# Score products in an attention kernel: operands stacked by copies over 128 rows, or used in place as two heads in the two halves of the array's rows

## The chip, the cores and the metric

One core of one Trainium2 chip. The metric is device time of one execution in microseconds (us), the median over runs. Engines are named as the profile names them: PE is TensorE (PEld its weight loads), DVE VectorE, ACT ScalarE, POOL GpSimd, SP the engine that issues the DMAs.

## The reference, cut to what matters

```python
# q, k, v: (8 batches, 8 heads, 576, 64);  tau = 0.02
def _attn_ref(q, k, v, tau):
    scores = np.matmul(q, k.transpose(0, 1, 3, 2)) / np.sqrt(64)
    thresh = np.max(scores, axis=-1, keepdims=True) - tau
    scores = np.where(scores >= thresh, scores, -1e9)
    attn = np.exp(scores - np.max(scores, axis=-1, keepdims=True))
    attn = attn / (np.sum(attn, axis=-1, keepdims=True) + 1e-09)
    return np.matmul(attn, v)

# x: attention output as (8, 576, 512);  w_k: 512x1024, w_v: 1024x512, w_r: 512x512
def _moe_ref(x, mu_k, mu_r, w_k, w_v, w_r):
    x_prev = x shifted by one position, zero first
    xk = mu_k * x + (1 - mu_k) * x_prev
    xr = mu_r * x + (1 - mu_r) * x_prev
    k = np.maximum(xk @ w_k, 0.0)
    return sigmoid(xr @ w_r) * (k * k @ w_v)
```

The threshold keeps only scores within tau of the row's maximum, so scores must be close to full f32.

## The kernel before, in words

**Two stages that overlap.** Attention goes batch by batch and, inside a batch, by pairs of heads (a "job", 36 in all: the first batch's four pairs are taken in two halves). A job's operands lie with the two heads above each other: the 64 numbers of head 0 on partitions 0 to 63, those of head 1 on 64 to 127. `raw` holds [q (576) | the last 64 keys | k (576)] for both, 1216 columns. A job has pair units, each 128 queries of both heads (128 such units over the run), and a last unit "T" with the remaining 64 queries of both heads (32 units). When a batch's attention is there, its feed-forward part runs in chunks of 256 positions (`ffn_chunk`: L853 the product with w_k, L895 with w_r, L917 with w_v).

**A pair unit** (`softmax`): the scores of the two heads go to two PSUM tiles `s`, of which there are two in all; then for each head the negated maximum (DVE, L555), the threshold (ACT, L563), exp (ACT, L571), the mask with its row sum (DVE, L579, the last reader of `s`), the reciprocal (DVE, L590), and the normalization (POOL, L604). PE then transposes the probabilities `p` (L628), ACT or DVE copies them to `pm` and `pl` (L646, L648), and `attend` multiplies with v (L708): the two heads write the two halves of the array's columns (128*64 in the profile), over 256 or 320 columns.

**Precision.** The matrix products run in fp32r, a rounded format. A number is split: `hi` is the rounded number (ACT, L434), `lo` the remainder (POOL, L440, in two pieces), and a product is hi.hi + hi.lo + lo.hi. In the feed-forward part these are three products over 128 rows. A head's scores have only 64 rows, so before the change `operands` makes stacked copies by DMA (L459, eight per job): `st1` has hi above lo, `st2` has lo above hi. Two products over 128 rows, st1.st1 and st2.st1, then hold all terms (lo.lo too). Each of them is done for two halves z of 288 keys: 4 products per head, 8 per unit, with one weight load each (L521). The T unit (L496) uses a block-diagonal `bd` and three products over 128 rows. The first job ("plain") multiplies `raw` in f32, 64 rows, head 0 in the upper and head 1 in the lower half of the array's rows (L510). An f32 product outside of transposes has two records in the trace, an fp32r product one.

**What sets the order.** The kernel adds steps to a `Plan`, each with an engine, an estimated time `occ`, a key, and what it reads and writes. `Plan.order` simulates the engines and buffers with these estimates and always places the step that can start first (ties by key; attention steps on PE have key - 1000, so they go before feed-forward steps that are also ready). The instructions are then issued in that order; each engine runs its own in order, and waits on semaphores where data or buffers are not ready. A step that writes two tiles is placed when both are free. Number of buffers per tile are those of `sbuf`/`psum`; `raw` has two, `s` two.

Of the kernel before, what the change touches and what calls it, by code (L numbers as in the profile page):

```python
# [8 lines left out]
F32 = mybir.dt.float32  # L9
FR = mybir.dt.float32r  # L10
# [38 lines left out]
class Plan:  # L49
# [18 lines left out]
    def add(self, eng, occ, fn, reads=(), writes=(), key=0.0, lat=None, kb=0, wait=0.0):  # L68
        s = Step()
        s.soft = self.SOFT.get(eng, 0.0) if self.soft else 0.0  # L70
        s.eng, s.occ, s.fn, s.key, s.kb = eng, occ, fn, key, kb
        s.lat = occ + 0.1 if lat is None else lat
        s.idx = len(self.steps)
        s.deps, s.succ, s.allocs = set(), [], []
        s.ready = wait

        def split(x):
            return x if isinstance(x, tuple) else (x, None)

        def near(b, r):  # L80
            if r is None:
                return list(b.regions.values())
            return [b.regions[x] for x in (r, None) if x in b.regions]

        for x in reads:
            b, r = split(x)
            for w, _ in near(b, r):
                s.deps.update(w)
        for x in writes:
            b, r = split(x)  # L90
            for w, rd in near(b, r):
                s.deps.update(w)
                s.deps.update(rd)
        for x in reads:
            b, r = split(x)
            b.regions.setdefault(r, ([], []))[1].append(s.idx)
            b.users.append(s.idx)
        for x in writes:
            b, r = split(x)
            if not b.users and b.make is None:  # L100
                self.tags.setdefault(b.tag, []).append(b)
            if r is None:
                b.regions = {None: ([s.idx], [])}
            else:

                b.regions[r] = ([s.idx], [])
            b.users.append(s.idx)
        s.deps.discard(s.idx)
        self.steps.append(s)
        return s  # L110
# [107 lines left out]
def tile_threshold_attention_then_rwkv_ffn(  # L218
# [12 lines left out]
    V, A, G, PE, SY = nc.vector, nc.scalar, nc.gpsimd, nc.tensor, nc.sync  # L231
# [3 lines left out]
    P = 128  # L235
    B, NPAIR, _, _ = qk.shape
    D = P // 2
    S = out.shape[1]
# [6 lines left out]
    HS = S // 2  # L245
    KT = S
    W = 2 * S + ST
# [11 lines left out]
    add = plan.add  # L259
    DQ = 0.55  # L260
    HALF = 1
    W0, W1, W2, W3, AVK = 3.0, 3.5, 50.0, 2.0, 4.5
    PREP, PB, VB, COLD, EARLY = 8, 2, 2, 24, 30
# [3 lines left out]
    def sbuf(tag, shape, dtype=F32, bufs=1):  # L267
        return plan.buf(sb, tag, shape, dtype, bufs)
# [4 lines left out]
    def fixed(name, shape, dtype=F32):  # L273
# [13 lines left out]
        writes=[(small, 0)],  # L287
        key=-100,
# [5 lines left out]
        reads=[(small, 0)],  # L294
        writes=[(small, 1)],
        key=-100,
# [5 lines left out]
        reads=[(small, 0)],  # L302
        writes=[(small, 2)],
        key=-100,
# [104 lines left out]
    def operands(job, key):  # L409
        b, hp = job["b"], job["hp"]  # L410
        raw = job["raw"] = sbuf("raw", [P, W], F32, 2)
        add("DMA", DQ, lambda: SY.dma_start(raw.get(), qk[b, hp]), writes=[raw], key=key - PREP - 5, kb=576)
        add(
            "ACT",
            0.67,
            lambda: A.activation(raw.get()[:, 0:S], raw.get()[:, 0:S], AF.Copy, scale=small.get()[:, 2:3]),
            reads=[(small, 2)],
            writes=[raw],
            key=key - PREP,
        )  # L420
        vt = job["v"] = sbuf("v", [P, 5, P], F32, VB)
        add(
            "DMA",
            DQ,
            lambda: SY.dma_start(vt.get(), v[b, hp].rearrange("p (c n) -> p c n", c=5)),
            writes=[vt],
            key=key - 5,
            kb=320,
        )
        if job["plain"]:  # L430

            return
        hi, lo = job["hi"], job["lo"] = sbuf("hi", [P, W], FR), sbuf("lo", [P, W], FR)
        add("ACT", 1.1, lambda: A.activation(hi.get(), raw.get(), AF.Copy), reads=[raw], writes=[hi], key=key - PREP)  # L434
        for y in range(2):
            cs = slice(0, S) if y == 0 else slice(S, W)
            add(
                "POOL",
                1.41 + 0.15 * y,
                lambda cs=cs: G.tensor_tensor(  # L440
                    lo.get()[:, cs], raw.get()[:, cs], hi.get()[:, cs].bitcast(F32), op=ALU.subtract
                ),
                reads=[raw, hi],
                writes=[(lo, y)],
                key=key - PREP,
            )
        job["st"] = [(sbuf("st1", [P, W], FR, 3), sbuf("st2", [P, S], FR, 3)) for _ in range(2)]
        for h in range(2):
            sl = slice(h * D, (h + 1) * D)
            t1, t2 = job["st"][h]  # L450

            up, dn = slice(0, D), slice(D, P)
            for dst, rows, src, n, r in (
                (t1, up, hi, W, (hi, None)),
                (t2, dn, hi, S, (hi, None)),
                (t1, dn, lo, W, (lo, None)),
                (t2, up, lo, S, (lo, 0)),
            ):
                fn = (lambda dst=dst, rows=rows, src=src, n=n, sl=sl: SY.dma_start(  # L459
                    dst.get()[rows, 0:n].bitcast(F32), src.get()[sl, 0:n].bitcast(F32)  # L460
                ))
                add("DMA", DQ, fn, reads=[r], writes=[(dst, rows.start)], key=key - PREP, kb=n // 4)

    def scores(unit, ss, key):
        job, c = unit["job"], unit["c"]
        raw = job["raw"]

        def keys(y, z):
            k0 = KT + (ST if unit["kind"] == "P" and y == 0 else 0)
            return slice(k0 + z * HS, k0 + (z + 1) * HS)

        if unit["kind"] == "T" and not job["plain"]:

            hi, lo = job["hi"], job["lo"]
            for v_, src in enumerate((raw, lo)):
                for h in range(2):
                    sl = slice(h * D, (h + 1) * D)  # L480
                    add(
                        "ACT",
                        0.26,
                        lambda v_=v_, src=src, sl=sl: A.activation(
                            bd.get()[sl, v_, sl], src.get()[sl, SM:S].bitcast(F32), AF.Copy
                        ),
                        reads=[(src, None if v_ == 0 else 0)],
                        writes=[(bd, (v_, h))],
                        key=key - 3,
                    )  # L490
            prods = [(0, hi), (0, lo), (1, hi)]
            for j, (v_, r) in enumerate(prods):

                def mm(j=j, v_=v_, r=r):
                    for z in range(2):
                        PE.matmul(ss[1].get()[:, z, 0:HS], bd.get()[:, v_], r.get()[:, keys(1, z)], start=(j == 0), stop=(j == 2))  # L496

                add("PE", 0.264, mm, reads=[bd, r], writes=[ss[1]], key=key - 1000, lat=0.44)
            return
        if unit["kind"] == "T" or job["plain"]:  # L500

            last = unit["kind"] == "T"

            def both():
                for z in range(2):
                    for h in range(2):
                        hr = slice(h * D, (h + 1) * D)
                        o = ss[1].get()[hr, z, 0:HS] if last else ss[h].get()[:, z, 0:HS]
                        q = slice(SM, S) if last else slice(c * P, (c + 1) * P)
                        PE.matmul(o, raw.get()[hr, q], raw.get()[hr, keys(h, z)], start=True, stop=True)  # L510

            occ = 1.2 if last or key > COLD else 3.0
            add("PE", occ, both, reads=[raw], writes=list(ss.values()), key=key - 1000, lat=occ + 0.25)
            return
        for y in range(2):
            st1, st2 = job["st"][y]
            for j, l in enumerate((st1, st2)):

                def mm(j=j, l=l, r=st1, y=y):
                    for z in range(2):  # L520
                        PE.matmul(  # L521
                            ss[y].get()[:, z, 0:HS],
                            l.get()[:, c * P : (c + 1) * P],
                            r.get()[:, keys(y, z)],
                            start=(j == 0),
                            stop=(j == 1),
                        )

                add("PE", 0.264, mm, reads=[l, st1], writes=[ss[y]], key=key + 0.5 * y - 1000, lat=0.44)

    def softmax(unit):
        n = unit["n"]
# [412 lines left out]
    n = 0  # L945
# [94 lines left out]
```

## Time and profile before

| | |
|---|---|
| median of 3 runs | 1096.16 us (1094.26 to 1098.05) |
| profiled execution, first to last instruction (span) | 1096.8 us; no other time is given for it |
| PE busy, products | 1024.5 us, 93%, 6832 records |
| DVE, ACT, POOL busy | 769.9, 736.4, 580.1 us |
| score products L521 | 1008 |
| copies by DMA L459 | 280, of 448 KB (hi or lo to both tiles of a head) in two pieces of 304 and 144 KB |
| all DMA traffic | 119.62 MB |

Products on PE overlap in the records: each has its start and a modelled end, so their pace is read from the starts. Rows of "PE in order of time" give start, length from the first start to the last end, the line, the shape of weights (rows*columns), the shape of the moving operand, and how many in a row. In rows of windows, after the window and its length, stand busy us (and count) of PE, PEld, DVE, ACT and POOL, then PE's granted clock, the share of the DMA engines and GB/s.

### The profile page before, as it was taken

How to read it: one execution, taken by the hardware profiler on the slowest of the kernel's cores; microseconds unless marked ns; L12 is line 12 of the kernel's file. 1: busy time of each engine (PE TensorE's matmuls, PEld its weight loads, DVE VectorE, ACT ScalarE, POOL GpSimd, SP SyncE). 2: the span in 40 equal slices, each digit the busy share in tenths (PEclk: the TensorE clock that was granted, in tenths of full speed). 3: DMA queues.
4: the chain of work that ended last, by engine and by line, in shares of the span. 5: the costliest groups of instructions: out<-in, count | busy, mean ns of one | idle time of the engine just before them, and what ended most of it. 6: DMA issues, size and time to landing. Idle time of an engine off the chain costs nothing.

```text
span 1096.8 us, 19388 instructions
## 1 busy us (share of the span) xinstructions
PE 1024.5 (93%) x6832; PEld 848.8 (77%) x6832; DVE 769.9 (70%) x1707; ACT 736.4 (67%) x1549; POOL 580.1 (53%) x584
## 2 busy tenths in 40 slices
PE   4667889998999999999999999999999999999998
PEld 3446667776878778788788878886888878888887
DVE  5999978877878788798877858855878488322220
ACT  5766977775876768777678767865777667344442
POOL 4667766544554555456545654654455544344441
PEclk9878999999999999999999999999999999999999
DMA  9994566444444444445444434530645141000000
GB/s 282 227 343 133 138 160 172 118 103 122 103 112 112 103 121 103 113 112 135 105 115 114 108 86 113 122 91 25 143 104 133 36 99 35 20 20 20 20 20 20
DMA packets 41279, 119.62 MB, mean 109 GB/s; under 512 B 6880, under 2 KB 6880, under 8 KB 41184
## 3 DMA queue, kind: packets, MB, share of 16 engines
q1 hardware_dynamic: 41184, 118.39, 41.6%
q8 instruction: 55, 0.90, 0.3%
q14 instruction: 40, 0.33, 0.1%
HBM read 44.70 MB, written 9.44 MB: 49 GB/s over the span
## 4 chain that ended last, share of the span: by engine, by line
PE 72%; DVE 12%; ACT 6%; DMA 5%; POOL 3%; issue 2%; SPq 0%; POOLq 0%; ACTq 0%; DVEq 0%
PE w L853 16%; PE w L917 14%; PE w L708 12%; PE w L628 10%; PE s L521 10%; PE w L895 8%; DMA st<-lo 3%; DVE p L579 3%; DVE mk L810 3%; DVE sm L555 2%; PE s L496 2%; ACT p L571 2%; DMA raw<-in_qk 2%; POOL lo L440 1%; DVE sm L589 1%
## 5 line engine op out<-in xcount | busy, mean ns | idle before, releaser
L604 POOL TENSOR_SCALAR p<-p,sm 128x576 f32<-128x576 f32 x288 | 223.1, 784 | 228.7 <-DVE sm L590 129.4
L579 DVE SCALAR_TENSOR_TENSOR p<-s,sm,p 128x576 f32<-128x576 f32 x288 | 232.8, 813 | 58.6 <-ACT p L571 56.4
L853 PE MATMUL w<-xk,wk 128*128 128x256 f32 x1728 | 237.8, 286 | 1.3 <-POOL xk L831 0.9
L555 DVE TENSOR_REDUCE sm<-s 128x1 f32<-128x576 f32 x288 | 210.8, 750 | 39.7 <-PE s L521 27.6
L853 PEld LDWEIGHTS w<-xk,wk 128*128 128x128 f32 x1728 | 219.4, 190 | 3.8 <-ACT pm L646 1.4
L917 PE MATMUL w<-wv,k 128*128 128x512 f32 x864 | 220.5, 396 | 1.6 <-ACT pm L646 1.5
L628 PE MATMUL w<-ident,p 128*128 128x128 f32 x1312 | 198.2, 283 | 22.6 <-POOL p L604 21.0
L571 ACT ACTIVATE p<-s,sm 128x576 f32<-128x576 f32 x288 | 210.1, 730 | 0.5
L628 PEld LDWEIGHTS w<-ident,p 128*128 128x128 f32 x1312 | 154.3, 144 | 62.0 <-POOL p L604 38.2
L917 PEld LDWEIGHTS w<-wv,k 128*128 128x128 f32 x864 | 155.8, 188 | 30.9 <-ACT pm L646 2.4
L646 ACT ACTIVATE pm<-w 128x512 f32<-128x512 f32 x174 | 102.5, 591 | 81.1 <-PE w L628 80.0
L831 POOL TENSOR_TENSOR xk<-mk,xk 128x512 fp32r<-128x512 f32 x72 | 94.9, 1318 | 104.8 <-ACT xk L823 104.7
L708 PE MATMUL w<-pm,v 128*64 128x256 f32 (+1 forms) x1024 | 144.8, 421 | 3.5 <-DVE pm L648 3.5
L563 ACT ACTIVATE sm<-sm,small 128x1 f32<-128x1 f32 x288 | 83.6, 290 | 93.7 <-DVE sm L555 90.7
L810 DVE SCALAR_TENSOR_TENSOR mk<-m,mu_sb,xT 128x256 f32<-128x256 f32 x128 | 87.2, 721 | 77.1 <-POOL xk L831 77.1
L521 PE MATMUL s<-st 128*128 128x288 f32 x504 | 119.6, 319 | 21.3 <-DVE p L579 15.3
L876 POOL TENSOR_TENSOR k<-r,k 128x512 fp32r<-128x512 f32 x72 | 93.7, 1302 | 71.1 <-ACT k L866 71.0
L440 POOL TENSOR_TENSOR lo<-raw,hi 128x576 fp32r<-128x576 f32 x70 | 105.6, 1526 | 43.6 <-ACT hi L434 36.2
L708 PEld LDWEIGHTS w<-pm,v 128*64 128x64 f32 x1024 | 71.0, 140 | 58.7 <-issue 9.0
L521 PEld LDWEIGHTS s<-st 128*128 128x128 f32 x504 | 82.0, 193 | 40.3 <-issue 25.5
L895 PE MATMUL w<-wr,xk 128*128 128x512 f32 x432 | 110.8, 396 | 1.6 <-ACT pm L646 1.6
L521 PE MATMUL s<-st,st 128*128 128x288 f32 x504 | 111.3, 303 | 0.0
(62 smaller groups left out, 1112.1 us busy)
## 6 DMA issues: line engine op xcount, KB each, us to landing
raw<-in_qk SPq DMA_DIRECT2D x36, 608.0 KB, 5.1
st<-hi SPq DMA_DIRECT2D x70, 304.0 KB, 3.2
st<-lo SPq DMA_DIRECT2D x70, 304.0 KB, 4.2
v<-in_v SPq DMA_DIRECT2D x36, 320.0 KB, 4.3
st<-hi SPq DMA_DIRECT2D x70, 144.0 KB, 3.5
st<-lo SPq DMA_DIRECT2D x70, 144.0 KB, 4.0
out<-sg SPq DMA_DIRECT2D x32, 256.0 KB, 2.0
wk<-in_w_k SPq DMA_DIRECT2D x8, 512.0 KB, 8.8
```

Of the source, the lines that this page charges most:

```text
L440: lambda cs=cs: G.tensor_tensor(lo.get()[:, cs], raw.get()[:, cs], hi.get()[:, cs].bitcast(F32), op=ALU.subtract),
L521: PE.matmul(ss[y].get()[:, z, 0:HS], l.get()[:, c * P : (c + 1) * P], r.get()[:, keys(y, z)], start=(j == 0), stop=(j == 1),)
L555: lambda sv=sv, col=col: V.tensor_reduce(col(0), sv(), axis=AX.XY, op=ALU.max, negate=True),
L571: lambda sv=sv, pv=pv, col=col: A.activation(pv(), sv(), AF.Exp, bias=col(0)),
L579: lambda sv=sv, pv=pv, col=col: V.scalar_tensor_tensor(pv(), sv(), col(1), pv(), op0=ALU.is_ge, op1=ALU.mult, accum_out=col(2)),
L604: lambda y=y: G.tensor_scalar(p.get()[:, y], p.get()[:, y], sm.get()[:, 3, y : y + 1], 0.0, op0=ALU.mult, op1=ALU.add),
L628: PE.transpose(pt.get()[:, c, :], p.get().rearrange("p y s -> p (y s)")[:, o : o + P], ident.get())
L708: PE.matmul(o.get()[hs, 0:n], vt.get()[:, c, hs], pt[:, 0:n], start=(c == 0), stop=(c == 4))
L810: V.scalar_tensor_tensor(d.get()[:, y, o : o + n], diff.get()[:, y, o : o + n], mu_sb.get()[:, j, hc + y : hc + y + 1], prv[:, hc + y], op ...
L853: PE.matmul(h.get()[:, f], l, r, start=(ct == 0 and i == 0), stop=(ct == NCT - 1 and i == 2))
L895: PE.matmul(z.get(), l, r, start=(ct == 0 and i == 0), stop=(ct == NCT - 1 and i == 2))
L917: PE.matmul(vps.get(), l, r, start=(ft == 0 and i == 0), stop=(ft == NFT - 1 and i == 2))
```

## The change: three products over 64 rows, both heads side by side

The copies go. The scores read `hi` and `lo` where they are; for each half z of the keys, three products per head, hi.hi, hi.lo and lo.hi, alternate between head 0 (partitions 0 to 63, the upper half of the array's rows) and head 1 (the lower half): 12 products with 12 weight loads per unit instead of 8, each over 64 rows. They are two steps (one per z) that each write both heads' `s` tiles, where there were four that wrote one. `hi` and `lo` get two buffers each in place of one, and the three `st1` and `st2` go. T units, the plain job and all else are as they were; the plan is computed anew, so the order changes everywhere.

```diff
-        hi, lo = job["hi"], job["lo"] = sbuf("hi", [P, W], FR), sbuf("lo", [P, W], FR)
+        hi, lo = job["hi"], job["lo"] = sbuf("hi", [P, W], FR, 2), sbuf("lo", [P, W], FR, 2)
...
-        job["st"] = [(sbuf("st1", [P, W], FR, 3), sbuf("st2", [P, S], FR, 3)) for _ in range(2)]
-        for h in range(2):
...
-                add("DMA", DQ, fn, reads=[r], writes=[(dst, rows.start)], key=key - PREP, kb=n // 4)
...
-        for y in range(2):
-            st1, st2 = job["st"][y]
-            for j, l in enumerate((st1, st2)):
-
-                def mm(j=j, l=l, r=st1, y=y):
-                    for z in range(2):
...
-                add("PE", 0.264, mm, reads=[l, st1], writes=[ss[y]], key=key + 0.5 * y - 1000, lat=0.44)
+        hi, lo = job["hi"], job["lo"]
+        qs = slice(c * P, (c + 1) * P)
+        for z in range(2):
+
+            def mm(z=z):
+                for j, (l, r) in enumerate(((hi, hi), (hi, lo), (lo, hi))):
+                    for h in range(2):
+                        hr = slice(h * D, (h + 1) * D)
                         PE.matmul(
-                            ss[y].get()[:, z, 0:HS],
-                            l.get()[:, c * P : (c + 1) * P],
-                            r.get()[:, keys(y, z)],
+                            ss[h].get()[:, z, 0:HS],
+                            l.get()[hr, qs],
+                            r.get()[hr, keys(h, z)],
                             start=(j == 0),
-                            stop=(j == 1),
+                            stop=(j == 2),
                         )
+            add("PE", 0.48, mm, reads=[hi, lo], writes=list(ss.values()), key=key - 1000, lat=0.66)
```

In the changed kernel the line numbers behind the cut are smaller by 16: L505 is the new score product, L510 becomes L492, L496 L478, L555 L539, L579 L563, L628 L612, L708 L692, L853 L837, L895 L879, L917 L901.

On PE in mid-kernel, two score blocks that follow each other, one of either head, before (`s_2874` and `s_2888` are the score tiles, `w` a PSUM tile of another product, `xk` the mixed input of the feed-forward part):

```order
L853 MATMUL w_2870<-xk_2308,wk_0_185 128x256 x3
L521 MATMUL s_2874<-st_2_2637 128x288 x2
L521 MATMUL s_2874<-st_2_2637,st_2_2648 128x288 x2
L853 MATMUL w_2870<-xk_2308,wk_0_217 128x256 x3
L521 MATMUL s_2888<-st_1_2452 128x288 x2
L521 MATMUL s_2888<-st_1_2452,st_1_2461 128x288 x2
L853 MATMUL w_2870<-xk_2308,wk_0_321 128x256 x3
```

The two heads stand apart, each as four products over the whole array. A unit in the same stretch of the changed kernel:

```order
L837 MATMUL w_2911<-xk_2133,wk_0_617 128x256 x3
L505 MATMUL s_2930<-hi_2438 128x288
L505 MATMUL s_2932<-hi_2438 128x288
L505 MATMUL s_2930<-lo_2450,hi_2438 128x288
L505 MATMUL s_2932<-lo_2450,hi_2438 128x288
L505 MATMUL s_2930<-hi_2438,lo_2450 128x288
L505 MATMUL s_2932<-hi_2438,lo_2450 128x288
```

The six rows of L505 come a second time, for the other z, and then L837 goes on. The two heads have moved together into one block that alternates between the halves.

On SP near its start, before (`wk` pieces of w_k, `raw` the operands of a coming job):

```order
L342 DMA wk_0_100<-in_w_k 128x512
L459 DMA st_0_109<-hi_103 64x1216
L459 DMA st_0_112<-hi_103 64x576
L459 DMA st_1_117<-hi_103 64x1216
L459 DMA st_0_112<-lo_107 64x576
L459 DMA st_1_124<-hi_103 64x576
L459 DMA st_1_124<-lo_107 64x576
L412 DMA raw_129<-in_qk 128x1216
```

The copies stand between the second piece of w_k and the third load of `raw`. In the changed kernel:

```order
L342 DMA wk_0_100<-in_w_k 128x512
L342 DMA wk_0_113<-in_w_k 128x512
L412 DMA raw_121<-in_qk 128x1216
L342 DMA wk_0_133<-in_w_k 128x512
L412 DMA raw_146<-in_qk 128x1216
L342 DMA wk_0_159<-in_w_k 128x512
```

Loads of weights and operands have moved into the places of the copies.

More of the change, by code (lines that the diff above doesn't have):

```diff
@@ L446, in operands @@
             )
-        job["st"] = [(sbuf("st1", [P, W], FR, 3), sbuf("st2", [P, S], FR, 3)) for _ in range(2)]
-        for h in range(2):
[L449 to L461, printed above, removed]
-                add("DMA", DQ, fn, reads=[r], writes=[(dst, rows.start)], key=key - PREP, kb=n // 4)
     def scores(unit, ss, key):
```

## The prediction

> **What bounds the kernel now.** I read the page first (engines, slices, chain), then the busy time by stages, then PE's waits, then PE in order of time.
>
> ```profile
> PE 1024.5 (93%) x6832; PEld 848.8 (77%) x6832; DVE 769.9 (70%) x1707; ACT 736.4 (67%) x1549; POOL 580.1 (53%) x584
> DMA  9994566444444444445444434530645141000000
> PE 72%; DVE 12%; ACT 6%; DMA 5%; POOL 3%; issue 2%; SPq 0%; POOLq 0%; ACTq 0%; DVEq 0%
> 0.00:10.00 10.00, 1.85 (x8) 1.18 (x8) 0.58 (x5) 3.93 (x4) 0.70 (x6) 1.00 0.75 261
> 10.00:60.00 50.00, 31.79 (x160) 22.72 (x160) 44.39 (x86) 35.39 (x72) 33.27 (x28) 0.90 0.96 263
> 60.00:110.00 50.00, 34.26 (x202) 26.40 (x198) 49.10 (x81) 31.92 (x67) 33.59 (x26) 0.83 0.73 225
> 150.00:930.00 780.00, 760.08 (x5298) 630.11 (x5297) 602.72 (x1381) 564.73 (x1232) 421.05 (x443) 1.00 0.43 108
> 930.00:1096.00 166.00, 161.72 (x967) 141.35 (x965) 38.39 (x90) 66.07 (x107) 64.86 (x60) 1.00 0.06 20
> ```
>
> The stage rows give window, length, then busy us of PE, weight loads, DVE, ACT and POOL, clock, DMA share and GB/s. Two stages differ. From 10 to 110 us the vector engine is full (44.4 and 49.1 of 50 us) and TensorE is not. From 150 us to the end TensorE is full (760 of 780, then 162 of 166), with DVE at 77% in the first of these. Busy time on PE covers modelled ends, so I check against PE's waits from 150 us on:
>
> ```profile
> PE w L628 <- POOL p L604: 4.9, 6, 1.2
> PE s L521 <- DVE p L579: 4.6, 6, 1.9
> ```
>
> These two are the largest; nothing here is waited for long. So from 150 us on, what is added to or taken from TensorE's stream is added to or taken from the time, nearly one for one, and the change must be counted on TensorE.
>
> **The products themselves.** One pair unit now has 8 score products of 288 columns, 504+504 = 1008 in 126 units. Two rows of the page have the counts; three of PE in order of time (start, length, line, count) give the pace, since products overlap and only the starts count:
>
> ```profile
> L521 PE MATMUL s<-st 128*128 128x288 f32 x504 | 119.6, 319 | 21.3 <-DVE p L579 15.3
> L521 PE MATMUL s<-st,st 128*128 128x288 f32 x504 | 111.3, 303 | 0.0
> ...
> 655.83 0.43 PE L521 MATMUL s<-st 128*128 128x288 f32 x2
> 656.09 0.43 PE L521 MATMUL s<-st,st 128*128 128x288 f32 x2
> 656.36 0.86 PE L917 MATMUL w<-wv,k 128*128 128x512 f32 x3
> ```
>
> From 655.83 to 656.36 four products start: 0.1325 us each, their weight loads hidden under the product before. Before: 126 x 8 x 0.1325 = 133.6 us.
>
> The change makes 12 products of 64 rows per unit, alternately in the upper and the lower half of the rows. Whether two of them share one step is shown by the first job, which has always worked that way (L510):
>
> ```profile
> 8.15 0.29 PEld L510 LDWEIGHTS s<-raw 64*128 64x128 f32 x2 [8.15 <-ACT raw L416]
> 8.15 0.85 PE L510 MATMUL s<-raw 64*128 64x288 f32 x2 [8.15 <-ACT raw L416]
> 8.15 1.33 PE L510 MATMUL s<-raw 64*128 64x288 f32 x4 [8.15 <-ACT raw L416]
> 8.15 2.29 PE L510 MATMUL s<-raw 64*128 64x288 f32 x8 [8.15 <-ACT raw L416]
> L510 PE MATMUL s<-raw x8: 681/684/847, 8.1 to 9.8; 64*128 64x288 f32 x8
> ```
>
> Two loads fit in 0.29 us and two products in 0.85 us, of which one alone is up to 847 ns long (last row: shortest, median, longest, ns): both started together, one in each half. Every further pair adds 0.48 (0.85, 1.33, then 2.29 for eight), so the halves kept pace, loads included. The steps are longer there: the operands are f32, whose 256-column pairs take 0.215 us in the rows below, and it is the first work of the run. So I take 6 steps of 0.1325 per unit: 100.2 us, a gain of 33.4 us.
>
> **What the change adds.** L708, the attention product, splits the array too, by columns (128*64), and shows what it costs to go from whole-array products to split ones and back:
>
> ```profile
> 651.34 0.42 PE L521 MATMUL s<-st,st 128*128 128x288 f32 x2
> 651.69 1.95 PE L708 MATMUL w<-pm,v 128*64 128x256 f32 x16
> 653.47 0.60 PE L708 MATMUL w<-pl,v 128*64 128x256 f32 x4
> 654.00 0.77 PE L628 MATMUL w<-ident,p 128*128 128x128 f32 x5
> 654.53 0.51 PE L521 MATMUL s<-st 128*128 128x288 f32 x2
> 654.88 0.43 PE L521 MATMUL s<-st,st 128*128 128x288 f32 x2
> 405.13 0.60 PE L708 MATMUL w<-pm,v 128*64 128x256 f32 x4
> 405.56 0.60 PE L708 MATMUL w<-pl,v 128*64 128x256 f32 x4
> 406.10 0.53 PE L521 MATMUL s<-st 128*128 128x288 f32 x2
> 406.47 0.42 PE L521 MATMUL s<-st,st 128*128 128x288 f32 x2
> 594.38 0.71 PE L628 MATMUL w<-ident,p 128*128 128x128 f32 x5
> 594.85 0.51 PE L521 MATMUL s<-st 128*128 128x288 f32 x2
> 595.20 0.43 PE L521 MATMUL s<-st,st 128*128 128x288 f32 x2
> ```
>
> - Entering. The two products at 651.34 take 0.35 us instead of 0.265 before L708 starts: 0.09 late. Sixteen L708 then take 1.78; at the steady pace (405.13 to 405.56, four in 0.43) they would take 1.72. So 0.06 more: the first weight load lies open.
> - Leaving. Four L708 at 405.56 take 0.54 instead of 0.43, and the next two L521 0.37 instead of 0.265: 0.11 and 0.11 (a 128-column load in the open). At 653.47 it is 0.10, and the transposes and products behind take 0.88 (654.00 to 654.88) where 594.38 to 595.20 shows 0.82: 0.06.
>
> So 0.15 into L708, 0.20 out to a weight product, 0.15 out to transposes. For a score block I take 0.09 plus an open load of 128 columns, 0.11: 0.20 in, and the same prices out. No row shows a row-split block entered from a busy array; L708 is the nearest one.
>
> How often? In the rows shown with the change, the blocks of the two heads were whole-array work among whole-array work (w<-xk,wk before, between and behind them) and cost no switch; now they are one block of split work between such products. Counting all of PE's order: 143 score blocks (109 of 12 products, 34 of 6, since 17 units have other work between their two z). 126 are entered from whole-array work and 17 from the attention product; 73 are left to weight products, 46 to transposes, 24 to the attention product. The attention product's own switches with whole-array work are 48 in, 7 out to weight products and 48 out to transposes; they were 65 in, 26 and 39 out.
>
> - Score blocks: 143 x 0.20 in, and out 73 x 0.20 + 46 x 0.15 + 24 x 0.15: 53.7 us.
> - Attention product: 48 x 0.15 + 7 x 0.20 + 48 x 0.15 = 15.8, before 65 x 0.15 + 26 x 0.20 + 39 x 0.15 = 20.8: -5.0 us.
>
> Switches +48.7, products -33.4: TensorE gets 15.3 us more work. There are 389 switches instead of 130; over the 259 more, 48.7 us is 0.19 each, and the change breaks even on TensorE at 33.4/259 = 0.13.
>
> The Trainium skill, page "TensorEngine Tiling (Array Packing)", section "Key Properties", says that changing the tiling mode drains TensorE; the trace agrees for column halves (0.09 to 0.11 us). The page gives no price for it, and does not speak of the open load, which is half of the sum.
>
> **What it removes.** 280 copies (four kinds, 70 each) leave SP's queue and the DMA engines. In the rows of SP shown with the change, weights and inputs move up to where the copies stood. The copies were waited for:
>
> ```profile
> 22.97 0.82 PE L521 MATMUL s<-st 128*128 128x288 f32 x2 [4.59 <-DMA st<-lo]
> PE s L521 <- DMA st<-lo: 0.7, 1, 0.7
> ```
>
> 4.59 us once at the start, 0.7 after 150 us. The 4.59 does not come free by itself: DVE works on through it, and holds 44.4 of the 50 us to 60 and 49.1 of the next 50, with the same softmaxes and weight pieces afterwards. What can be won is DVE's idle time from 10 to 60 us, 5.6 us. I take 4; bounds 0 and, should PE's idle time of this stage follow more freely, 12. ACT, POOL and DVE keep every instruction, and hi and lo get a second buffer in place of the three st pairs, so operands are prepared as early as before.
>
> **The wait it adds.** A unit's products now write both score buffers, and there are two: no head can start while a mask of the unit before runs, and TensorE's queue stands behind it. Row L579 above says 4.6 us for the old form. Bounds: -4.6 (all gone) to twice the old, +5, or far more if the plan's times are off (rival 2). I take 0, because every block takes longer on PE than it used to, so the masks gain on it.
>
> Sum against the profiled execution's span of 1096.8: +15.3 - 4 = 1108.1. The median of the runs is 0.6 lower, so 1107.5.
>
> **Rivals.** 1. *Switching into row halves is cheaper.* With 0.09 a switch and loads hidden, 259 x 0.09 = 23.3: -33.4 + 23.3 - 4 = -14, 1082. For it: L708 splits columns, not rows, and its loads are of other shapes; L510's loads of two halves went side by side. Against: four rows of L708 all show an open load. It decides below 0.13 a switch, or 37.4/259 = 0.14 with the start. Beside it stands a page of the Trainium skill, "TensorE: Matmul & The Clock Gate", Part 2: a drain is about 128 cycles at 2.4 GHz, as an estimate 0.05 us; by that 259 switches cost 13 us, and the time would be 1073. The trace shows 0.09 for the drain alone.
> 2. *Both score buffers at once.* A PE wait on a mask costs 4.6/6 = 0.77 us; if one unit in three has one, 42 x 0.77 = 32: 1140. For it: PE is in order. Against: 1024.5 us of PE over 160 units (128 pairs of heads, 32 last rows) is 6.4 us of other work per unit for a mask to end in.
> 3. *The halves do not pair at this pace.* L510 steps are longer than 0.1325; if the two loads of 0.11 must follow each other, a pair takes 0.22, 756 x 0.0875 = +66: 1174. If products don't overlap at all, 756 more steps of 0.1325, +100 on top of the sum: 1208. Against: L510's pairs.
>
> **Chances.** Forecast 0.57, rival 1 0.26, rival 2 0.10, rival 3 0.07. The range 1080 to 1134 leaves out rival 3, some of rival 2 and the cheapest end of rival 1, together 0.17; the forecast's own is 1097 to 1120. A change of under 0.3% (3.3 us) can't be told from none: faster 0.25, same 0.09, slower 0.66.
>
> **What the next profile would show.** L505 x1512, starting in pairs, 12 in about 0.8 us; the product ahead of each block followed 0.09 late, and about 0.2 lost on leaving; PE as full as before from 150 us; DVE's idle time from 10 to 60 us nearly gone; no st. I am wrong if the product behind a block starts at the normal pace, if the pairs take 0.2 us a step, or if PE waits for L563 (the mask) in many units.

## The result, and the profile after

The changed kernel takes 1155.96 us (median of 4 runs, 1155.23 to 1156.7), the kernel before 1095.38: ratio 1.0545, interval 1.0528 to 1.0563. It is slower by 60.6 us; the forecast was 1107.5, its range ended at 1134. The profiled execution has a span of 1153.5 us.

The page of the changed kernel, in the order in which the old one was read: busy time and counts, PE and its clock over 40 slices, the chain that ended last.

```profile
PE 1056.4 (92%) x7336; PEld 833.7 (72%) x7336; DVE 790.7 (69%) x1707; ACT 740.0 (64%) x1553; POOL 583.8 (51%) x584
PE   4677988997999889998899999999999999999998
PEclk9878999998999989998899999999999999999999
PE 70%; DVE 16%; ACT 8%; POOL 3%; issue 2%; DMA 0%; POOLq 0%; SPq 0%; ACTq 0%
```

DMA has left the chain (it had 5%), and DVE and ACT have taken more than its place. In the first half the clock dips at regular distances (slices 9, 14 and 18 to 19, the first slice being 0), and PE with it. The stages (columns as before):

```profile
10.00:60.00 50.00, 30.91 (x164) 22.25 (x162) 47.34 (x86) 34.33 (x71) 33.97 (x28) 0.90 0.46 165
60.00:110.00 50.00, 36.42 (x236) 25.91 (x236) 47.88 (x88) 38.29 (x82) 35.86 (x29) 0.86 0.41 152
150.00:930.00 780.00, 732.81 (x5257) 575.12 (x5258) 555.47 (x1222) 514.78 (x1104) 392.76 (x403) 0.97 0.12 39
930.00:1096.00 166.00, 163.91 (x1129) 133.59 (x1128) 96.21 (x214) 94.98 (x193) 78.69 (x81) 1.00 0.06 19
```

From 150 to 930 us PE is idle for 47 us (780 - 732.8; before 19.9), at a clock of 0.97 instead of 1.00. And DVE has done 1222 of its instructions where it had done 1381: the softmax is behind, and 214 of them are left for the stage after 930, where there were 90. What PE waits for after 150 us, and who waits for PE in the whole run (us in total, times, longest; then groups of instructions):

```profile
PE s L478 <- DVE p L563: 23.3, 10, 5.6
PE w L612 <- POOL p L588: 10.0, 21, 1.4
PE s L505 <- DVE p L563: 9.4, 13, 1.5
```

```profile
L539 DVE TENSOR_REDUCE sm<-s 128x1 f32<-128x576 f32 x288 | 205.8, 751 | 101.5 <-PE s L505 88.1
L505 PE MATMUL s<-hi 64*128 64x288 f32 x504 | 103.1, 361 | 27.8 <-DVE p L563 27.8
```

```profile
L555 DVE TENSOR_REDUCE sm<-s 128x1 f32<-128x576 f32 x288 | 210.8, 750 | 39.7 <-PE s L521 27.6
```

The first two blocks are of the changed kernel, the last line is the same maximum in the kernel before. PE waits for masks 32.7 us after 150 us (23.3 + 9.4), where it was one row of 4.6. The other way round, DVE's maximum waits 88.1 us for the scores of pair units instead of 27.6. Each side now stands and waits for the other. Attention has become slower: a batch has 36 masks, and the 72nd, 108th and 144th start at 278.4, 414.9 and 551.7 us, before at 257.0, 363.4 and 474.6. A batch there takes 137 us instead of 106 to 111.

The longest of these waits, in order of time (T unit L478, mask L563, w_k product L837, maximum L539, exp L555, lo L440; mk and xk are the feed-forward part's next input, made on DVE, ACT and POOL):

```profile
272.73 0.30 PE L505 MATMUL s<-hi,lo 64*128 64x288 f32 x2
273.06 1.42 DVE L539 TENSOR_REDUCE sm<-s 128x1 f32<-128x576 f32 x2 [0.41 <-PE s L505]
274.38 3.07 POOL L440 TENSOR_TENSOR lo<-raw,hi 128x576 fp32r<-128x576 f32 x2 [1.90 <-ACT hi L434]
274.40 3.34 DVE L794 SCALAR_TENSOR_TENSOR mk<-m,mu_sb,xT 128x256 f32<-128x256 f32 x2
274.40 0.72 ACT L555 ACTIVATE p<-s,sm 128x576 f32<-128x576 f32 x1
277.66 0.81 DVE L563 SCALAR_TENSOR_TENSOR p<-s,sm,p 128x576 f32<-128x576 f32 x1
278.48 1.28 POOL L815 TENSOR_TENSOR xk<-mk,xk 128x512 fp32r<-128x512 f32 x1 [1.02 <-ACT xk L807]
278.62 0.82 PE L478 MATMUL s<-hi,bd 128*128 128x288 f32 x2 [5.60 <-DVE p L563]
280.19 2.12 PE L837 MATMUL w<-xk,wk 128*128 128x256 f32 x9
```

```profile
272.00:275.60 3.60, 1.02 (x13) 0.79 (x12) 3.19 (x4) 2.91 (x7) 1.70 (x2) 1.00 0.00 0
275.60:282.40 6.80, 3.78 (x17) 3.81 (x18) 6.28 (x12) 2.99 (x9) 4.60 (x5) 0.50 0.13 33
```

Both heads' scores end at 273.03, both score tiles are taken, and the next scores can start only when a mask lets go of one, at 278.62. Nothing else could have run on PE: the w_k products behind read an xk that POOL finishes at 279.76. The wait is one of a whole batch's boundary: the feed-forward work of the batch before is used up, and attention alone is left, one unit's chain at a time (scores, two maxima, two exps, two masks, next scores). Part of it isn't that chain: the first exp ends at 275.12, but DVE's order has two L794 for the feed-forward part ahead of the mask, which starts 2.5 us later. They take 3.34 us together, beside L440 on POOL, where one takes 0.785 on the mean. No run moves them behind the masks. The wait comes again at 415 and 552 us, a batch later each time, with the same 3.34 us ahead of the mask; the three make 16.8 of the 32.7 us. The clock falls to half in the 6.8 us around its end and behind it. The Trainium skill, "TensorE: Matmul & The Clock Gate", Part 1, says that after about one idle window of some 3.4 us TensorE's clock is halved, and that a busy window of that length brings it back; the trace agrees in part: 0.50 over 6.8 us follows 5.60 us of waiting, but PE was busy for 1.02 of the 3.6 us ahead of the drop, and from 401.9 us on the clock is at half for 3.4 us after a stretch as long in which PE was busy for 2.25 us, with no wait near it over 1.50.

**An account of PE's stream.** For every product I took the time from its start to the next start, less the steady step of its shape (0.1325 for a whole score product or a pair of halves, 0.118, 0.2285, 0.109 for the others, 0.1065 or 0.133 for each record of L692/L708, which start in pairs). What is over at a change between whole and split array counts as switch up to 0.11 on either side of it, in stretches of half clock as slow clock, the rest as wait. After 150 us, in us (the number of switches in brackets):

| kernel | score products | other products | switches | waits | slow clock | sum |
|---|---|---|---|---|---|---|
| before | 142.2 | 741.2 | 17.3 (108) | 37.8 | 3.1 | 941.7 |
| after | 111.2 | 741.8 | 59.5 (336) | 68.9 | 17.0 | 998.4 |
| after less before | -31.0 | +0.6 | +42.2 (228) | +31.1 | +13.9 | +56.7 |

The rest of the stream, 142 us in both, lies ahead of 150 us; it is that long by its definition, whatever was done in it.

### The profile page after: what moved, and what is told of

It is laid out like the page before. It is cut to its first block, busy times and chain, and to the rows that moved or that the text cites. A ratio compares the mean times of both kernels' runs of the same rounds, so it can differ in the third digit from the quotient of the medians.

```text
span 1153.5 us, 19707 instructions
## 1 busy us (share of the span) xinstructions
PE 1056.4 (92%) x7336; PEld 833.7 (72%) x7336; DVE 790.7 (69%) x1707; ACT 740.0 (64%) x1553; POOL 583.8 (51%) x584
## 4 chain that ended last, share of the span: by engine, by line
PE 70%; DVE 16%; ACT 8%; POOL 3%; issue 2%; DMA 0%; POOLq 0%; SPq 0%; ACTq 0%
PE w L837 18%; PE w L692 13%; PE w L612 10%; PE w L901 10%; PE s L505 10%; PE w L879 8%; DVE p L563 4%; DVE sm L539 3%; DVE mk L794 3%; ACT p L555 3%; PE s L478 2%; POOL p L588 2%; DVE sm L573 1%; ACT hi L434 1%; ACT L555 1%
## 5 line engine op out<-in xcount | busy, mean ns | idle before, releaser
L588 POOL TENSOR_SCALAR p<-p,sm 128x576 f32<-128x576 f32 x288 | 228.0, 801 | 264.2 <-DVE sm L574 257.0
L563 DVE SCALAR_TENSOR_TENSOR p<-s,sm,p 128x576 f32<-128x576 f32 x288 | 232.5, 814 | 67.5 <-ACT p L555 64.7
L539 DVE TENSOR_REDUCE sm<-s 128x1 f32<-128x576 f32 x288 | 205.8, 751 | 101.5 <-PE s L505 88.1
L837 PE MATMUL w<-xk,wk 128*128 128x256 f32 x1728 | 244.7, 291 | 2.6 <-ACT pm L630 2.6
L837 PEld LDWEIGHTS w<-xk,wk 128*128 128x128 f32 x1728 | 219.0, 192 | 11.7 <-issue 6.5
L901 PE MATMUL w<-wv,k 128*128 128x512 f32 x864 | 221.4, 400 | 3.5 <-ACT pm L630 1.8
L612 PE MATMUL w<-ident,p 128*128 128x128 f32 x1312 | 200.4, 286 | 21.5 <-POOL p L588 20.7
L555 ACT ACTIVATE p<-s,sm 128x576 f32<-128x576 f32 x288 | 211.0, 733 | 0.2
L612 PEld LDWEIGHTS w<-ident,p 128*128 128x128 f32 x1312 | 153.8, 145 | 69.1 <-POOL p L588 42.1
L901 PEld LDWEIGHTS w<-wv,k 128*128 128x128 f32 x864 | 156.6, 188 | 38.0 <-issue 4.6
L692 PE MATMUL w<-pm,v 128*64 128x256 f32 (+1 forms) x1024 | 149.1, 427 | 0.5 <-DVE pm L632 0.3
L440 POOL TENSOR_TENSOR lo<-raw,hi 128x576 fp32r<-128x576 f32 x70 | 106.0, 1534 | 66.7 <-ACT hi L434 59.4
L505 PE MATMUL s<-hi 64*128 64x288 f32 x504 | 103.1, 361 | 27.8 <-DVE p L563 27.8
L794 DVE SCALAR_TENSOR_TENSOR mk<-m,mu_sb,xT 128x256 f32<-128x256 f32 x128 | 95.4, 785 | 40.9 <-POOL xk L815 40.9
L879 PE MATMUL w<-wr,xk 128*128 128x512 f32 x432 | 114.1, 404 | 0.0
L692 PEld LDWEIGHTS w<-pm,v 128*64 128x64 f32 x1024 | 73.8, 142 | 54.0 <-issue 10.3
L505 PEld LDWEIGHTS s<-hi 64*128 64x128 f32 x504 | 56.0, 191 | 69.1 <-issue 54.4
L632 DVE COPY pm<-w 128x512 f32<-128x512 f32 x114 | 78.4, 688 | 26.6 <-PE w L612 25.9
```

The source lines that it names most:

```text
L440: lambda cs=cs: G.tensor_tensor(lo.get()[:, cs], raw.get()[:, cs], hi.get()[:, cs].bitcast(F32), op=ALU.subtract),
L505: PE.matmul(ss[h].get()[:, z, 0:HS], l.get()[hr, qs], r.get()[hr, keys(h, z)], start=(j == 0), stop=(j == 2),)
L539: lambda sv=sv, col=col: V.tensor_reduce(col(0), sv(), axis=AX.XY, op=ALU.max, negate=True),
L555: lambda sv=sv, pv=pv, col=col: A.activation(pv(), sv(), AF.Exp, bias=col(0)),
L563: lambda sv=sv, pv=pv, col=col: V.scalar_tensor_tensor(pv(), sv(), col(1), pv(), op0=ALU.is_ge, op1=ALU.mult, accum_out=col(2)),
L588: lambda y=y: G.tensor_scalar(p.get()[:, y], p.get()[:, y], sm.get()[:, 3, y : y + 1], 0.0, op0=ALU.mult, op1=ALU.add),
```

## Experiments

The theory after the result: the products and the switches cost what the prediction says, and the rest comes from the step that writes both score tiles (theory "joint"). The expectations call it theory B; their theory A is that the switches are what the change costs. Other rivals: the switches cost far more than 0.19 each; the plan's too short time for the new step (0.48) or an unlucky order; the loss of the copies. Several kernels compute other scores; what each leaves out stands in its expectation.

### Taking the change apart: the first four kernels

**e1**, the changed kernel with each pair of halves replaced by one product over all rows, in the same order:

```diff
-                    for h in range(2):
-                        hr = slice(h * D, (h + 1) * D)
-                        PE.matmul(ss[h].get()[:, z, 0:HS], l.get()[hr, qs], r.get()[hr, keys(h, z)], ...)
+                    h = j % 2
+                    PE.matmul(ss[h].get()[:, z, 0:HS], l.get()[:, qs], r.get()[:, keys(h, z)], ...)
```

> The changed kernel with its order kept, but a unit's 12 products over 64 rows issued as 6 over all 128 rows (three per z, hi.hi and lo.hi into one head's tile, hi.lo into the other's), so the scores mix heads and lack terms. No score block splits the array any more; both score tiles are still written by one step. Theory A (the switches between whole-array and split work, priced at 0.20 in and 0.15 to 0.20 out, are what the change costs): about 1156 - 49 = 1107 or lower, to 1095 if the waits of PE go too. Theory B (one step that needs both score tiles slows attention, PE runs dry and its clock falls): 1135 to 1150, with the long PE waits on the mask still there. Rival 3 of the prediction (the halves don't pair): not seen in the trace, 12 products took six steps of 0.133.

Measured: 1128.93 us, ratio 1.0276 (1.0252 to 1.03). At the same order and the same pace of products, the switches are worth 27 us (1155.96 - 1128.93), less than their 42 us on PE, since waits grow when they go (82.2 us in PE's account, with them 68.9). The greater part of the loss, 31 us, is there without any split, though PE has 32 us less of score products than before. The time lies between the ranges of the two theories, and each has a part.

**e2**, the kernel before, copies and all, but with two steps per unit (one per z) that write both tiles, in place of four that write one:

```diff
-        for y in range(2):
-            st1, st2 = job["st"][y]
-            for j, l in enumerate((st1, st2)):
-                ... for z in range(2): PE.matmul(ss[y].get()[:, z, 0:HS], ...)
-                add("PE", 0.264, mm, ..., writes=[ss[y]], ...)
+        for z in range(2):
+                ... for j in range(2): for y in range(2): PE.matmul(ss[y].get()[:, z, 0:HS], ...)
+            add("PE", 0.528, mm, ..., writes=list(ss.values()), ...)
```

> The kernel before, copies and whole-array products kept, 8 per unit, but issued as two steps (one per z) that each write both heads' score tiles, as the change does. No switch is added and no product removed. Theory A: 1095 plus or minus 5. Theory B: 1120 to 1140, PE waits on the mask of 20 us and more from 150 us on, slow clock windows after them.

Measured: 1198.63 us, ratio 1.0914 (1.0889 to 1.0938): +101 us with the same products and hardly a switch more (116 after 150 us, before 108), far above theory B's 1120 to 1140. Two rows of its waits, over the whole run, and its stage from 150 us:

```profile
DVE sm L554 <- PE s L520: 76.7, 80, 3.7
PE s L520 <- DVE p L578: 38.1, 31, 7.1
150.00:930.00 780.00, 722.93 (x4775) 595.63 (x4775) 539.66 (x1191) 509.64 (x1090) 385.05 (x396) 0.97 0.39 97
```

The same pattern as in the changed kernel: both sides wait, PE is idle for 57 of 780 us, the clock is at 0.97, DVE is behind (1191 instructions). The +101 isn't the joint step's price alone: a unit here needs all eight copies before its first product, and the start is worse as well (in the first 150 us PE is busy 91.1 us, before 102.7).

**e3**, the kernel before in exactly its order, with head 1's products over the upper 64 rows only, so that the array switches and nothing else changes:

```diff
-                            l.get()[:, c * P : (c + 1) * P],
-                            r.get()[:, keys(y, z)],
+                            l.get()[0 : D if y else P, c * P : (c + 1) * P],
+                            r.get()[0 : D if y else P, keys(y, z)],
```

> The kernel before with its order kept instruction for instruction; head 1's products read only the upper 64 rows of the stacked operands, so its scores lack terms. Each takes the same step, but its blocks now split the array: 361 switches on PE instead of 130. Theory A: 231 more at 0.19, about +43, 1139. Theory B: within 5 us of before, since no step needs more tiles than it did; then the price of a switch in the trace is somehow hidden.

Measured: 1127.91 us, ratio 1.0285 (1.0246 to 1.0325): +30 us for 231 switches, 0.13 each in the time. On PE's stream after 150 us they take 39.8 us more for 211 more, 0.19 each; waits fall by 11.6 us, and the slow clock grows by 7.7 (the profiled execution took 1135.74 us, 7.8 more than the median). So the price of a switch is as predicted, and the time takes only a part of it: theory A's 1139 isn't reached, theory B's 5 us are far exceeded.

**e5**, no copies, the heads apart as before, eight whole products that read hi and lo in place (two buffers of each, as in the change):

```diff
-            st1, st2 = job["st"][y]
+            st1, st2 = job["hi"], job["lo"]
```

> The kernel before without the 280 copies: the 8 whole-array products of a unit read hi and lo as they lie (two buffers each), so the heads mix; steps per head, each with its own score tile, as before. It takes away the copies alone. The prediction's term: -4 (0 to -12), 1091. If the first 150 us are bound by the vector engine whatever the copies do, as the trace of the changed kernel suggests (PE did the same work in its first 150 us as before): 1093 to 1097.

Measured: 1112.95 us, ratio 1.0128 (1.0102 to 1.0154). Taking the copies out doesn't bring 4 us, it costs 15; after 150 us waits are 12.4 us longer than before (50.2).

### The plan and the tiles' release

**e4**, the changed kernel with the plan told a longer time for the step (`0.48` to `0.59`, latency `0.66` to `0.77`).

> The changed kernel with the plan told what a score step really takes on PE (0.59 us per z with its switch, instead of 0.48). Instructions as in the change, order planned anew. Theory A (switches): PE's work is the same, 1150 to 1160. Theory B (joint score tiles): attention is bound by its own chain, which the estimate does not shorten, 1145 to 1165. A third view, that the long waits come from a plan made with a wrong cost: 1120 to 1135.

Measured: 1161.18 us, ratio 1.0579 (1.0563 to 1.0595). A truer time in the plan gives nothing back.

**e6**, the changed kernel with a mask that reads the probabilities in place of the scores, so that a score tile is free after exp; **e7**, the same in the kernel before, and **e8**, in the changed one, both with the threshold taken once for all rows (exp of -tau):

```diff
-                    pv(), sv(), col(1), pv(), op0=ALU.is_ge, op1=ALU.mult, accum_out=col(2)
+                    pv(), pv(), col(1), pv(), op0=ALU.is_ge, op1=ALU.mult, accum_out=col(2)
```

> The changed kernel, but the mask (second pass of the vector engine) compares the exponentials in SBUF instead of the scores, with the old threshold left as it was, so it keeps every element: the last reader of a score tile is now the exp, and both tiles come free one or two masks earlier (0.8 us each, more where other work stands between). Every instruction and all switches stay. Theory B: a batch of attention falls from about 130 to 110 us and the time to 1105 to 1125, PE's waits for score tiles go to under 10 us from 150 us on. Theory A: 1145 to 1156, since the switches are all there.

> The kernel before with the mask taken from the exponentials: p >= exp(-tau), the constant made once, in place of s >= max - tau. The 288 small threshold instructions on ACT go (84 us of ACT), the score tiles come free one mask earlier. No copies or products change. PE is the bound from 150 us on and waited 4.6 us for score tiles there, so Theory A expects 1085 to 1096 (the start alone). Theory B, by which attention's chain sets how well PE is fed, expects 1065 to 1085.

> The same edit on the changed kernel (three products over 64 rows, no copies, both score tiles in one step). Theory B: with the chain shorter the joint step costs little, and what is left against the kernel before with the same edit is switches less products, +15: 1085 to 1105. Theory A: 1125 to 1150.

Measured: e6 1168.51 us (1.0644, 1.0625 to 1.0662), e7 1142.02 (1.0406, 1.0385 to 1.0426), e8 1165.08 (1.0621, 1.0604 to 1.0637). They don't tell the theories apart, since the new mask costs more itself. Two groups of e6, then one of e7:

```profile
L563 DVE SCALAR_TENSOR_TENSOR p<-p,sm 128x576 f32<-128x576 f32 x288 | 296.0, 1041 | 79.0 <-ACT p L555 74.0
L588 POOL TENSOR_SCALAR p<-p,sm 128x576 f32<-128x576 f32 x288 | 235.6, 828 | 257.6 <-DVE sm L574 212.7
```

```profile
L604 POOL TENSOR_SCALAR p<-p,sm 128x576 f32<-128x576 f32 x288 | 242.7, 853 | 215.6 <-DVE sm L590 180.6
```

The mask takes 1041 ns, 814 before: 288 x 0.227 = 65 us more on DVE. What can be read from e6 all the same: PE's waits for score tiles after 150 us fell from 32.7 to 12.6 us (9.6 at L505 and 3.0 at L478, both now on the exp), so it is the mask's hold on the tiles that PE waits for. And e8 lies 23 us above e7, where the change lies 61 us above the kernel before: with tiles that are free after exp the change costs less, as theory B has it, though the slower mask weighs on both.

### Joint or apart, and what a shorter PE is worth

**e9**, as e5, with six whole products in place of eight, the heads apart: as many whole products as in e1, without the joint step.

```diff
-                    for z in range(2):
+                    for z in range(2 - j):
...
-                add("PE", 0.264, mm, ..., writes=[ss[y]], key=key + 0.5 * y - 1000, lat=0.44)
+                add("PE", 0.264 / (1 + j), mm, ..., writes=[ss[y]], key=key + 0.5 * y - 1000, lat=0.18 + 0.264 / (1 + j))
```

> No copies, 6 whole-array products per unit (hi and lo as they lie, three per head, so terms are missing and heads mix), but steps per head that each write one score tile, as in the kernel before. Against the kernel with the joint step and the same 6 products (1129 us) only the joining of the heads differs, and the order that follows from it. Theory B (the joint step makes waits of about 45 us and a slow clock of 14): 1075 to 1090. If instead the waits come from any new plan: 1115 or more.

Measured: 1095.24 us, ratio 0.9965 (0.9948 to 0.9983). Against e1 (1128.93) that is 34 us for joining the heads and for the order that the plan makes of it, with the same number and shape of products, the same buffers, and no copies in either. It is just above theory B's range (1075 to 1090) and far below the 1115 of its rival. Waits for scores and the stages, e9 first, then e1:

```profile
DVE sm L536 <- PE s L502: 16.2, 35, 2.2
150.00:930.00 780.00, 747.76 (x5093) 612.39 (x5092) 622.77 (x1374) 567.18 (x1221) 425.36 (x441) 0.99 0.13 41
```

```profile
DVE sm L538 <- PE s L504: 66.2, 89, 1.8
150.00:930.00 780.00, 725.58 (x4818) 591.41 (x4817) 576.26 (x1262) 534.45 (x1145) 409.02 (x420) 0.97 0.13 40
```

With the heads apart DVE waits 16.2 us for scores and has done 1374 instructions by 930 us; joined, 66.2 and 1262. In PE's account the waits go from 56.6 to 82.2 and the slow clock from 7.2 to 17.4: 25.6 + 10.2 = 36 us. From the 72nd to the 144th mask, two batches, the time is 208 us apart and 263 joined.

**e12**, the kernel before in exactly its order, with six of its eight products:

```diff
-                    for z in range(2):
+                    for z in range(2 - j):
```

> The kernel before in its own order, copies and all, with 6 of the 8 products of a unit issued (the second product is left out for one z, so terms are missing). TensorE is freed of 33 us and nothing else moves. The prediction's premise, that from 150 us on PE's work counts nearly one for one: 1064 to 1070. If waits fill half of it: 1080.

Measured: 1085.26 us, ratio 0.9886 (0.9861 to 0.9912): -13.5 us, a smaller fall than either figure of the expectation. The account shows 30.5 us less of score products and 17.0 us more of waits.

```profile
150.00:930.00 780.00, 753.35 (x5149) 608.80 (x5148) 608.59 (x1397) 570.54 (x1244) 429.11 (x451) 1.00 0.43 108
```

PE's busy time falls only from 760.1 to 753.4 in this stage, and DVE gets little further (1397 instructions, before 1381): other waits take over at once.

**e10** and **e11** are the kernel before with a new order alone: the plan's time of a score step `0.264` to `0.27`, and a plan constant for late steps `0.3` to `0.4`.

> The kernel before, same instructions, with the plan's estimate of a score step at 0.27 us instead of 0.264, so that the order is computed anew. A control for what a new order does by itself: within 1% of before, 1087 to 1108. If a new plan alone made the waits of the change: 1130 or more.

> A second control: the kernel before with the plan's lateness of attention steps on PE at 0.4 us instead of 0.3. Same instructions, another order: 1087 to 1108; 1130 or more if any new plan makes such waits.

Measured: 1097.74 us (0.9999, 0.9984 to 1.0013) and 1095.53 (0.9982, 0.9965 to 0.9999). A reshuffled order by itself moves the time by 0.2% at most in these two cases; nothing of the size of the 15 to 100 us of the other kernels is seen.

### Why reading in place costs 15 us

**e14** is e5 with three buffers of hi and lo in place of two; **e15** is e5 with the copies issued all the same, into tiles that nobody reads.

> The kernel before without copies (8 whole-array products that read hi and lo as they lie, heads apart), with three buffers of hi and lo instead of two. Without copies a buffer is held until the job's last scores are done. If the 15 us that the copies' removal cost come from operands that are prepared too late or at a bad time for want of a buffer: 1090 to 1102. If the buffers don't matter: 1108 to 1116.

> The same two-buffer kernel without copies in its products, but the 280 copies are issued all the same into tiles that nobody reads. If the copies' absence from the DMA engines and SP matters in any way (or their presence costs): away from 1113, towards 1098 or above 1116. If the scores' reading of hi and lo in place is what costs: 1108 to 1116.

Measured: 1111.02 us (1.0129, 1.0112 to 1.0147) and 1107.95 (1.0102, 1.0066 to 1.0138). Buffers aren't the cause, and the copies' traffic gives back 3 to 5 us of the 15, if that. What is seen in e5, e9 and the changed kernel is that some operations on DVE are longer. L794 of the changed kernel, which was 721 ns long before (L810):

```profile
L794 DVE SCALAR_TENSOR_TENSOR mk<-m,mu_sb,xT 128x256 f32<-128x256 f32 x128 | 95.4, 785 | 40.9 <-POOL xk L815 40.9
```

DVE is busy 790.7 us there and 795.9 in e5, before 769.9. The length of L794 comes from what stands beside it: it takes 477 ns in each of these kernels when POOL is idle beside it (under 5% of its time), and 904 (before) to 969 (after) when POOL works throughout (over 90%); 62 of the 128 ran beside an idle POOL before, 42 in the changed kernel. It doesn't explain the 15 us: in e15 L794 is back at 724 ns, and the time is still 1107.95. The cause of the 15 us stays open.

### The sum of the parts

From the kernel before (1097 to 1099 beside these runs): no copies +15 (e5), six products instead of eight -18 (e9), heads joined +34 (e1), halves instead of whole rows +27 (after): 58 together, where the change costs 60.6. None of the kernels with the whole computation is faster than the one before by more than can be told from no change; e9 and e12, which leave terms out, aren't versions of it.

## Why the prediction was wrong

**The products: right.** Halves pair: a block of 12 among w_k products, PE in order of time:

```profile
626.25 1.10 PE L837 MATMUL w<-xk,wk 128*128 128x256 f32 x8
627.28 0.40 PE L505 MATMUL s<-hi 64*128 64x288 f32 x2
627.52 0.29 PE L505 MATMUL s<-lo,hi 64*128 64x288 f32 x2
627.65 0.29 PE L505 MATMUL s<-hi,lo 64*128 64x288 f32 x2
...
628.05 0.30 PE L505 MATMUL s<-hi,lo 64*128 64x288 f32 x2
628.28 0.63 PE L837 MATMUL w<-xk,wk 128*128 128x256 f32 x3
628.74 0.49 PE L612 MATMUL w<-ident,p 128*128 128x128 f32 x3
```

From 627.52 to 628.05 four pairs start, 0.1325 us each. The gain is 31.0 us after 150 us and 2.4 in the first 150 (20.7 to 18.3); forecast 33.4. Rival 3 is out.

**The switches: right.** Eight w_k products at 626.25 take 1.03 us, at 0.118 it would be 0.94: 0.09 late on entering. The first pair takes 0.24 instead of 0.13: the open load, 0.11. On leaving, the last pair takes 0.23 (0.10 more), and three w_k products behind it 0.46 instead of 0.35: 0.11. That is the forecast's 0.20 in and 0.20 out, read there from L708. Over the run there are 390 switches (forecast 389), and the 228 more after 150 us cost 0.185 each (forecast 0.19). Rival 1 is out.

**The copies: wrong in sign.** The 4.59 us wait for st is gone, and the softmax starts out ahead: the 36th mask, the last of the first batch, starts at 149.7 us instead of 157.7, in e5 at 148.2. But PE has as much left to do at 150 us (741.8 us of other products, before 741.2), DVE is as full as it was (47.3 and 47.9 of 50 us), and nothing of the lead is left further on: the 72nd mask is late, by 21 us in the changed kernel and 10 in e5. In the time the bound 0, not 4, would have been nearer, and e5 shows a loss of 15 us that was in no term; its cause is open.

**The failed step: "The wait it adds ... I take 0".** The sentence behind it was that the blocks take longer on PE, so the masks gain on it. It looked at PE alone. With one step for both tiles the next unit's scores can't be made while a unit is in its softmax, nor one head's softmax run while the other's scores are made, so DVE stands as well (88.1 us instead of 27.6), and attention falls behind the feed-forward part that lives on its output (137 us for a batch instead of 106 to 111). At three batches' ends PE then has no other work: waits of up to 5.6 us, and the half clock after them. The bounds -4.6 to +5 were taken from the old row of waits, which is the row of a kernel whose two tiles are released apart; it says nothing of a step that needs both. Rival 2 had the mechanism, with a chance of 0.10 and 32 us; waits are 31.1 us longer, and the slow clock, which no term had, adds 13.9. That 32 and 31.1 lie so close is luck: the rival took 42 waits of 0.77 us, and there are 23 on masks, 1.4 us on the mean. By e9 against e1 the joint step, with the order planned for it, is worth 34 us. The argument against rival 2, 6.4 us of other work per unit, was an average over the run, and the longest waits stand where there is none.

**A second premise failed: "nearly one for one".** It was read from PE's 97% from 150 us on. e12 took 30.5 us of work from PE and the time fell by 13.5; e3 added 39.8 and it rose by 30. So something else stood close behind PE; that it is attention's chain is argued, not shown by these two. In the account the 48 us by which the forecast was too low come out nearly whole: of +15.3 expected on PE, +11.8 came (42.2 + 0.6 - 31.0), the -4 of the start did not come, and the waits and the clock added 45.0. That makes 45.5; the profiled executions lie 56.7 us apart, the medians 60.6.

## What to carry to other kernels

A step that needs several buffers at once takes away the overlap that these buffers were there for: before joining steps, follow one unit's chain through all engines and ask what runs in the meantime, at the place with the least other work, not on the average. An engine that is 97% busy tells what is full, not what a shorter step there is worth; the next chain may be just behind it, and one kernel with the work left out (e12) shows it in one run. And count the switches of array mode: here 0.185 us each, so splitting pays only in blocks long enough to earn two of them.

## What the runs showed of the hardware

- A switch to row halves cost what the prediction read from column halves: 0.09 to 0.10 us more for the product ahead of it, and 0.11 for the first load of 128 columns, in the open, each way.
- Products in the two halves of the rows pair at 0.1325 us for 288 columns, the pace of one whole product, with their two loads side by side.
- The mask with both operands in SBUF took 998 to 1055 ns (e7, e6, e8) in place of 814 with one in PSUM, and POOL's normalization beside it 828 to 853 instead of 784 (before) and 801 (after). The Trainium skill, "GPSIMD Engine Reference", section "Specifications", says that GpSimd shares its SBUF interfaces with VectorE and that instructions there with two SBUF inputs contend for them; the trace agrees, and gives 3 to 9% on POOL and 23 to 30% on DVE. With POOL idle the mask of e6 took 814 ns (160 of 288), with POOL at work throughout 1486 (55); the old mask took 814 and 815.
- Waits of PE cost more than their length: 31.1 us more of waiting came with 13.9 us more of slow clock.
